# Induced attention and a leaky feed-forward layer on one core: another order of the opening list, the next batch's first loads sent from within it, and longer pauses in two lanes

## The chip, the core and the metric

The kernel runs on one core of a Trainium2 chip. A time is in device microseconds from the start to the end of one execution, and the number to predict is the median of several runs. TensorE multiplies, VectorE and ScalarE work on what it leaves in PSUM, GpSimd does a few elementwise steps, and the queue of SyncE (SP) issues nearly all DMAs, one after the other in the order of the program.

## What is computed

```python
def _attn_ref(x, inducing):              # x (4, 12480, 128), inducing (32, 128)
    def mab(q, kv):
        s = scale * (q @ kv.transpose(0, 2, 1))
        s = s - s.max(-1, keepdims=True)
        a = np.exp(s)
        a /= a.sum(-1, keepdims=True) + 1e-09
        return a @ kv
    h = mab(I, x)                        # 32 rows for each batch
    return mab(x, h)

def _moe_ref(x, w_in, w_out):            # x: the 49920 rows of the attention; w_in (128, 2048), w_out (2048, 128)
    h = x @ w_in
    g = np.maximum(0.01 * h, h)
    return g @ w_out
```

## The kernel before

**Feed-forward part.** The 49920 rows are cut into tiles of 512 tokens, a few of them put together from remainders. For each tile and each of 16 parts of the hidden width there is one *slot*: TensorE makes `ph` from the tile's attention weights `A` and the batch's expanded weights `hws` (L712), ScalarE writes its upper part `ghi` (L725), VectorE what is left over, `glo` (L733), and TensorE adds three products to `po` (L751). After the last part of a tile comes one closing product (L770), then VectorE turns `po` into `osb` (L780), for the first four tiles GpSimd scales it (L783), and SP stores it with four DMAs (L804). `ph` has three buffers, so the `ph` of slot u+3 cannot start before the `glo` of slot u is read out.

**Attention part of a batch.** Per batch there are seven groups of rows: six of 2048 and a remainder of 192. `first_scores` loads blocks `xc` with 32x32 pieces (L250, eight DMAs for a block of half a group, twelve for the remainder; three buffers), VectorE transposes them into `xT` (L391, L397), TensorE scores them against the inducing rows (L264). `fetch` loads the rows `xr` (L222), which give `h` (L440). From `h` come `hws` (L547 to L562) and the second scores; `second` makes their softmax `y` into `aT`, and `stack` splits `aT` into `ahi` (ScalarE, L641) and `alo` (L646) and spreads them with 16 DMAs over four tiles of `A` (L658). There are six `A` buffers: a stack goes on only when its tiles fit beside those still held.

**What sets the order.** Batch 0 up to slot 50 is written by hand: the table `ORDER` names one step after the other, and `start` runs them in that order. `T`, `C` turn and copy a quarter of a group; `S`, `M`, `X`, `N`, `E`, `Y`, `Z`, `H` are scores, maxima, exponentials and products of the first attention; `a`, `b`, `o`, `t`, `p` with a number convert a piece of the raw weights, and `sh`, `sl`, `wt`, `wc`, `wm`, `wd` derive weights from it; `hw`, `wh`, `wl`, `hd` make `hws`; `F`, `G`, `L`, `A`, `B` with a slot's number are `ph`, `ghi`, `glo`, the first and the other two products; `dA2`, `dA3` spread tiles 2 and 3; `os0` to `os2` store a tile; the names that end in `1` (`ymx1` to `yT1`) are the softmax of the second group, and `ah1`, `alo1v`, `dB` drive its stack; `yg2`, `ygR` turn scores of groups 2 and R; `W` is a warm-up product for TensorE's clock (L1217). Tiles 0 and 1 take turns every four slots, so that tile 0 ends with `B27` and tile 1 with `B31`.

From slot 48 on a loop runs the slots and beside them *lanes*, generators that each do a step when their turn comes: stores, `stacking`, `fetches`, `seconds`, `scores` (`first_scores`) and `values`. A step that yields `HEAVY` (15) makes a debt that each slot lowers by 4 or 5, and most lanes wait while there is one. Steps of `fetches` come every second slot. `first_scores` of batch 1 therefore sends its first loads when the loop has begun. `idle(n)` yields n times and does nothing.

All engines execute in the order in which they were written. SP does too: a DMA whose buffer is not free holds all that are behind it.

Of the kernel before, what the change touches and what calls it, by code (L numbers as in the profile page):

```python
# [9 lines left out]
F32 = mybir.dt.float32  # L10
# [10 lines left out]
def induced_attention_then_leaky_ffn(  # L21
# [21 lines left out]
    B, N, C = x.shape  # L43
# [12 lines left out]
    while N - base >= 4 * TOK:  # L56
# [15 lines left out]
    STEPS = [[0, 1, 2], [3, 4], [5, RG]]  # L72

    ORDER = """
        W W W W W indT W W W W T0.1 C0.1v W T0.0 C0.0v W W W T0.2 C0.2a W T0.3 T1.0 C0.3v C1.0v T1.1
        C1.1v S0 M0 T1.3 C1.3a T2.0 T1.2 C1.2v T2.1 C2.0v T2.2 T2.3 C2.3v C2.1a S1 C2.2a S2 M1 T3.1 T3.0
        C3.1a T3.2 M2 X0 C3.2a N0 E0 E2 C3.0v T3.3 T4.1 C3.3v C4.1a T4.2 T4.0 Y0 C4.0v T4.3 C4.2a TR.0 S3
        C4.3a t0 CR.0v S4 E1 a0 M3 T5.0 b0 T5.1 T5.2 M4 X1 Z0 Y1 N1 C5.0a C5.1a T5.3 SR C5.2a al1 H0 o0
        MR C5.3a b1 Y2 a1 o1 p0 S5 t1 p1 H1 H2 M5 X2 E3 Y3 t2 K0 W E4 N2 E5 ER Y4 b2 H3 Y5 H4 a2 Z1 a3
        al2 H5 o2 p2 Z2 z YR K1 HR rz a4 wt1 t3 K2 sr hT t5 b3 hTc b4 o3 p3 s2 o4 sg2 hw y ymx ysubv t4  # L80
        p4 a5 wt0 wt3 wc1 wh wl s21 yex wc0 wm0 yT ah W b5 alov wc3 rep0 rep1 W sh0 J0 J1 o5 ysm hd0 hd1
        hd2 y1 F0 G0 L0 F1 G1 wd0 F2 L1 G2 L2 p5 wm1 sh1 A0 F3 sl0 B0 G3 F4 A1 B1 F5 G4 G5 sl1 A2 a6 L3
        B2 A3 F6 G6 L4 L5 dA3 B3 F7 A4 B4 wt2 ysr G7 L6 L7 t6 A5 B5 b6 F8 wc2 F9 G8 o6 G9 p6 F10 A6 B6 A7
        A8 G10 b7 a7 L8 L9 L10 B7 F11 B8 A9 G11 F12 B9 G12 sc sq A10 B10 L11 L12 F13 o7 G13 t7 A11 A12
        B11 F14 wm2 L13 F15 F16 ymx1 G14 B12 wd1 A13 L14 G15 L15 G16 F17 G17 L16 p7 L17 B13 A14 B14 wm3
        A15 F18 F19 sh2 A16 yg2 G18 sl2 G19 L18 L19 B15 B16 F20 A17 G20 wd2 F21 G21 ysub1g B17 A18 B18
        A19 A20 sh3 F22 B19 G22 L20 L21 B20 A21 wd3 m2 F23 L22 G23 L23 hd3 F24 G24 F25 B21 A22 G25 B22
        L24 sgR F26 mh G26 ml F27 G27 A23 L25 yex1 B23 A24 F28 G28 L26 sl3 B24 A25 F29 B25 G29 A26 B26
        A27 A28 L27 L28 F30 F31 G30 B27 G31 B28 A29 ysm1 L29 L30 dA2 F32 os0 B29 G32 L31 F33 G33 L32 L33
        ysr1 A30 B30 A31 A32 F34 F35 B31 B32 A33 G34 L34 F36 B33 A34 G35 L35 G36 F37 G37 L36 F38 B34 A35  # L90
        B35 A36 L37 F39 F40 G38 L38 G39 L39 B36 F41 G40 G41 A37 L40 B37 A38 B38 A39 F42 F43 G42 G43 L41
        B39 A40 F44 G44 B40 A41 B41 L42 L43 F45 G45 F46 A42 L44 L45 B42 G46 F47 A43 B43 A44 L46 B44 F48
        A45 B45 G47 L47 G48 A46 L48 F49 F50 G49 L49 G50 ymul1g os1 yT1 ah1 alo1v dB B46 A47 B47 os2 L50
        ygR
    """.split()

    QUICK = 2
# [13 lines left out]
    def aux_ps(name):  # L111
        return ps_a.tile([P, TOK], F32, tag="aux", name=name)
# [13 lines left out]
    indT = const.tile([P, M], F32, tag="indT", name="indT")  # L126
# [5 lines left out]
    scores, early, ready, summed = [], {}, set(), {}  # L132
# [4 lines left out]
    xT, xr, ex, aT, A4, hw, maxima, sums_of = {}, {}, {}, {}, {}, {}, {}, {}  # L137
# [88 lines left out]
    def fetch(b):  # L226

        for p, gs in enumerate(PASSES):
            while p and (b, 1) not in visited:
                yield  # L230
            for g in gs:
                for q in range(max(1, GROUPS[g][2] // 4)):
                    while not room():
                        yield
                    load_rows(b, g, q)
                    yield

    def landed(b, p):

# [388 lines left out]
    def stack(tiles_, engine=None):  # L628

        while len(A4) + len(tiles_) > A4_BUFS or not all(s[:2] in aT for t in tiles_ for s in t[1]):  # L630
            yield
        ahi = sb.tile([P, TOK], F32R, tag="ahi", name="ahi", bufs=1)
        alo = sb.tile([P, TOK], F32R, tag="alo", name="alo", bufs=1)
        at = {}
        for _, parts in tiles_:
            for b, g, *_ in parts:
                if (b, g) not in at:
                    at[b, g] = sum(32 * GROUPS[q][2] for _, q in at)
        for (b, g), o in at.items():
            _, J, K = GROUPS[g]  # L640
            nc.scalar.copy(ahi[: 32 * J, o : o + 32 * K], aT[b, g][: 32 * J, :])  # L641
        yield
        for (b, g), o in at.items():
            _, J, K = GROUPS[g]
            sl = (slice(0, 32 * J), slice(o, o + 32 * K))
            (engine or nc.gpsimd).tensor_tensor(  # L646
                out=alo[sl], in0=aT.pop((b, g))[: 32 * J, :], in1=ahi[sl].bitcast(F32),
                op=ALU.subtract,
            )
        yield  # L650
        for t, parts in tiles_:
# [184 lines left out]
    def start(stacking, seconds, chosen):  # L836
# [377 lines left out]
        def warm():  # L1214
# [137 lines left out]
```

## Time and profile before

| | us |
|---|---|
| median of three runs | 1508.52 |
| the runs | 1505.11 to 1508.65 |
| profiled execution | 1507.05 |
| its span | 1505.1 |
| TensorE busy | 1484.8 |
| VectorE busy | 1265.1 |
| ScalarE busy | 997.6 |
| SP: `xc` loads | 288 of 64 KB and 36 of 8 KB |

The span is from the first to the last instruction. The page gives busy times and shares; the timelines give single instructions with, in brackets, how long the engine had been idle before one and what ended that; the table by windows gives busy time and the clock that TensorE was granted (1.00 is 2.4 GHz, 0.50 is 1.2 GHz; a value between is a mean over the window).

### The profile page before, as it was taken

The numbers are of one execution on the slowest core, as the hardware profiler recorded it, in microseconds if no ns is written. First come the engines' busy times: TensorE is split into PE (matmuls) and PEld (weight loads), VectorE is DVE, ScalarE is ACT, GpSimd is POOL, SyncE is SP. The second block draws the span as 40 slices with busy tenths as digits, with TensorE's granted clock in tenths as the row PEclk, the third lists the DMA queues.
The fourth block names the chain that finished last, engine by engine and source line by source line (L and its number), as shares of the span: only waits on it lengthen the run. The fifth ranks groups of instructions, "written<-read, shape, count | busy, mean of one in ns | idle before, by whom it ended". The sixth has DMA issues, their size and how long they took to land.

```text
span 1505.1 us, 22252 instructions
## 1 busy us (share of the span) xinstructions
PE 1484.8 (99%) x7863; PEld 1264.3 (84%) x7863; DVE 1265.1 (84%) x2128; ACT 997.6 (66%) x1746; POOL 116.9 (8%) x186
## 2 busy tenths in 40 slices
PE   8997999999999999999999999999999999999998
PEld 6786888888888888888888888888888898888887
DVE  7886898879898898788899898788888888888886
ACT  5764676667676676676676676676766766666665
POOL 1310000001000000010000000010100000000000
PEclk9998999999999999999999999999999999999999
DMA  8126536434544452244533531221212212212211
GB/s 283 43 50 122 95 60 144 90 47 96 92 90 81 95 108 50 46 84 69 117 64 64 147 61 25 43 64 29 50 27 43 39 31 45 44 25 46 41 28 21
DMA packets 402079, 105.23 MB, mean 70 GB/s; under 512 B 372624, under 2 KB 375088, under 8 KB 401968
## 3 DMA queue, kind: packets, MB, share of 16 engines
q1 hardware_dynamic: 401920, 103.80, 34.2%
q8 instruction: 62, 1.02, 0.3%
q14 instruction: 49, 0.40, 0.1%
q10 hardware_dynamic: 48, 0.02, 0.0%
HBM read 48.94 MB, written 25.56 MB: 49 GB/s over the span
## 4 chain that ended last, share of the span: by engine, by line
PE 94%; DMA 2%; SPq 1%; DVE 1%; ACT 1%; issue 0%; DVEq 0%; ACTq 0%
PE po L751 66%; PE ph L712 22%; PE s_ps L264 2%; PE po L770 1%; DMA xr<-in_x_dram 1%; PE h_ps L440 1%; SPq L250 1%; DMA xc<-in_x_dram 0%; DVE glo L733 0%; PE hw_ps L547 0%; ACT ghi L725 0%; PE h_ps L985 0%; PE w_ps L1085 0%; SPq L658 0%; DVE osb L780 0%
## 5 line engine op out<-in xcount | busy, mean ns | idle before, releaser
L725 ACT ACTIVATE ghi<-ph 128x512 fp32r<-128x512 f32 (+1 forms) x1568 | 928.9, 595 | 475.4 <-PE ph L712 470.6
L733 DVE SCALAR_TENSOR_TENSOR glo<-ph,ghi 128x512 fp32r<-128x512 f32 (+1 forms) x1568 | 1041.5, 679 | 187.5 <-ACT ghi L725 165.4
L712 PE MATMUL ph<-A,hws 128*128 128x512 f32 (+1 forms) x1600 | 596.9, 378 | 10.0 <-DVE glo L733 8.5
L751 PE MATMUL po<-ghi,w_hi 128*128 128x512 f32 (+1 forms) x1568 | 594.4, 380 | 0.4 <-DVE osb L780 0.4
L751 PE MATMUL po<-glo,w_hi 128*128 128x512 f32 (+1 forms) x1568 | 594.2, 379 | 0.0
L751 PE MATMUL po<-ghi,w_lo 128*128 128x512 f32 (+1 forms) x1568 | 594.1, 379 | 0.0
L712 PEld LDWEIGHTS ph<-A,hws 128*128 128x128 f32 x1600 | 302.4, 189 | 70.0 <-DVE glo L733 14.4
L751 PEld LDWEIGHTS po<-ghi,w_lo 128*128 128x128 f32 x1568 | 297.1, 189 | 41.5
L751 PEld LDWEIGHTS po<-glo,w_hi 128*128 128x128 f32 x1568 | 297.2, 190 | 41.3
L751 PEld LDWEIGHTS po<-ghi,w_hi 128*128 128x128 f32 x1568 | 297.1, 189 | 40.5 <-issue 0.8
L780 DVE STREAM_TRANSPOSE osb<-po 128x512 f32<-128x512 f32 (+1 forms) x98 | 68.9, 703 | 1.5 <-PE po L770 1.5
L646 POOL TENSOR_TENSOR alo<-aT,ahi 128x512 fp32r<-128x512 f32 x22 | 28.5, 1296 | 488.2 <-ACT ahi L641 449.0
L397 DVE STREAM_TRANSPOSE xT<-xc 128x512 f32<-128x512 f32 x72 | 50.5, 701 | 8.0 <-DMA xc<-in_x_dram 8.0
L599 POOL TENSOR_TENSOR y<-y,mx 128x512 f32<-128x512 f32 x23 | 24.2, 1052 | 245.4 <-DVE mx L597 220.3
L614 POOL TENSOR_TENSOR y<-y,sm 128x512 f32<-128x512 f32 x23 | 24.2, 1051 | 183.7 <-DVE sm L612 154.8
L770 PE MATMUL po<-A,m2s 128*128 128x512 f32 (+1 forms) x100 | 37.4, 377 | 0.0
L357 DVE STREAM_TRANSPOSE y<-s_ps 128x512 f32<-128x512 f32 x22 | 15.8, 717 | 10.8 <-PE s_ps L264 9.2
L264 PE MATMUL s_ps<-xT,indT 128*32 128x512 f32 x192 | 24.1, 595 | 0.0
L264 PE MATMUL s_ps<-xT,hT 128*32 128x512 f32 x192 | 23.8, 596 | 0.4 <-ACT hT L1029 0.4
L770 PEld LDWEIGHTS po<-A,m2s 128*128 128x128 f32 x100 | 19.0, 190 | 2.6
L282 DVE TENSOR_SCALAR_CACHE_REDUCE e<-s_ps 128x512 f32<-128x512 f32 x18 | 12.4, 691 | 8.3 <-PE s_ps L264 7.5
L440 PE MATMUL h_ps<-xr,ay 128*32 128x128 f32 x576 | 17.6, 274 | 0.0
(161 smaller groups left out, 378.3 us busy)
## 6 DMA issues: line engine op xcount, KB each, us to landing
xr<-in_x_dram SPq DMA_DIRECT2D x96, 256.0 KB, 4.8
out_dram<-osb SPq DMA_DIRECT2D x384, 64.0 KB, 2.2
xc<-in_x_dram SPq DMA_DIRECT2D x288, 64.0 KB, 2.7
A<-ahi SPq DMA_DIRECT2D x188, 64.0 KB, 2.0
A<-alo SPq DMA_DIRECT2D x188, 64.0 KB, 2.0
hws<-hilo SPq DMA_DIRECT2D x64, 64.0 KB, 2.0
raw<-in_moe_w_in_dram SPq DMA_DIRECT2D x4, 512.0 KB, 7.6
raw<-in_moe_w_out_dram SPq DMA_DIRECT2D x4, 512.0 KB, 9.2
```

The lines of the kernel that those rows point to most:

```text
L264: nc.tensor.matmul(dst, lhsT, rhs, start=True, stop=True)
L397: nc.vector.transpose(t[:, j, :], blk.rearrange("p n c -> p (n c)"))
L440: nc.tensor.matmul(hp[32 * k : 32 * k + 32, :C], ay[:rows, 4 * q + k, :], xb[:rows, k, :], start=(i == 0 and q == 0), stop=(last[k] == i a ...
L599: engines[0].tensor_tensor(out=yv, in0=yv, in1=mx[:rows, :K].unsqueeze(2).broadcast_to([rows, K, M]), op=ALU.subtract,)
L614: engines[1].tensor_tensor(out=yv, in0=yv, in1=smv.unsqueeze(2).broadcast_to([rows, K, M]), op=ALU.mult)
L646: (engine or nc.gpsimd).tensor_tensor(out=alo[sl], in0=aT.pop((b, g))[: 32 * J, :], in1=ahi[sl].bitcast(F32), op=ALU.subtract,)
L712: nc.tensor.matmul(ph[:, o : o + w], hw[b][1][:, f * P : (f + 1) * P], woven(A4[t][:, o : o + w], t), start=True, stop=True,)
L725: nc.scalar.activation(halves(ghi[:, :n], t)[1], live[u][2], AF.Relu)
L733: nc.vector.scalar_tensor_tensor(out=halves(glo[:, :n], t)[1], in0=ph, scalar=0.0, in1=halves(ghi[:, :n], t)[1].bitcast(F32), op0=ALU.max, ...
L751: nc.tensor.matmul(accs[t][:, :n], w[:, f, :], woven(r[:, :n], t), start=(f == 0 and w is w_hi and r is live[u][0]), stop=False,)
L770: nc.tensor.matmul(accs[t][:, o : o + w], hw[b][2], woven(a4[:, o : o + w], t), start=False, stop=(o + w == n),)
L780: nc.vector.transpose(osb[:, :n], po[:, :n])
```

## The change

Four edits. The table `ORDER` is written anew from its first row to its last. A new name in it, `pf`, takes the first step of `first_scores` of batch 1, which sends the loads of its first three blocks; so that it can, the generators are made ahead of `start`. `fetch` yields twice after a load instead of once, and `stack` fourteen times at its end instead of three. The numbers of lines after the table are one lower than before.

```diff
@@ ORDER, its end @@
-        A45 B45 G47 L47 G48 A46 L48 F49 F50 G49 L49 G50 ymul1g os1 yT1 ah1 alo1v dB B46 A47 B47 os2 L50
-        ygR
+        A44 B44 A45 F47 F48 G47 L47 B45 A46 G48 F49 B46 A47 L48 F50 G49 G50 B47 L49 os1 L50 ygR os2
@@ ORDER, its middle @@
+        pf mh ml ah1 B27 G28 L28 G29 G30 L29 L30 F31 F32 A28 B28 G31 sq os0 A29 B29 alo1v A30 F33 L31 G32
+        A35 L36 L37 B35 A36 F39 F40 G39 L38 L39 B36 A37 B37 A38 F41 G40 L40 G41 F42 L41 dB B38 A39 B39
@@ fetch @@
                     load_rows(b, g, q)
-                    yield
+                    yield from idle(2)
@@ stack @@
                     to += w
                 yield
-        yield from idle(3)
+        yield from idle(14)
@@ plain @@
+            "pf": lambda: next(scores[0]),
@@ main @@
         stores, values = [], []
+        scores += [first_scores(b) for b in range(1, B)]
         start(stacking[1], seconds[:2], chosen)
         del stacking[:2], seconds[:2]
-        scores += [first_scores(b) for b in range(1, B)]
```

SP, from the spreads of tile 3 to the loop's first blocks, before. `A_1310` is the first tile of the second stack; its 16 spreads are cut after two.

```order
L1172 DMA A_1115<-alo 32x512
L804 DMA out_dram<-osb 512x1x32 x8
L658 DMA A_1310<-ahi 32x512
L658 DMA A_1310<-alo 32x512
...
L804 DMA out_dram<-osb 512x1x32 x4
L250 DMA xc<-in_x_dram 32x2x32 x12
L250 DMA xc<-in_x_dram 32x16x32 x16
L222 DMA xr<-in_x_dram 96x256
L222 DMA xr<-in_x_dram 128x512 x6
L804 DMA out_dram<-osb 512x1x32 x4
L222 DMA xr<-in_x_dram 128x512 x2
L250 DMA xc<-in_x_dram 32x16x32 x16
```

The same stretch of SP in the changed kernel.

```order
L1171 DMA A_907<-alo 32x512
L249 DMA xc<-in_x_dram 32x2x32 x12
L249 DMA xc<-in_x_dram 32x16x32 x16
L803 DMA out_dram<-osb 512x1x32 x4
L657 DMA A_1258<-ahi 32x512
L657 DMA A_1258<-alo 32x512
...
L803 DMA out_dram<-osb 512x1x32 x8
L221 DMA xr<-in_x_dram 96x256
L221 DMA xr<-in_x_dram 128x512 x3
L803 DMA out_dram<-osb 512x1x32 x4
L221 DMA xr<-in_x_dram 128x512
L249 DMA xc<-in_x_dram 32x16x32 x8
```

The 28 loads of the first three blocks have moved ahead of three tiles' stores and of the second stack, and the stores of tiles 1 and 2 behind the stack.

VectorE, from the first tile's store to the end of the list, before (`osb` of tiles 0, 1 and 2; `yr` is the remainder's second score).

```order
L780 STREAM_TRANSPOSE osb<-po 128x512
L733 SCALAR_TENSOR_TENSOR glo<-ph,ghi 128x512 x3
L611 TENSOR_SCALAR sm<-sm 128x16
L612 RECIPROCAL sm<-sm 128x16
L733 SCALAR_TENSOR_TENSOR glo<-ph,ghi 128x512 x16
L780 STREAM_TRANSPOSE osb<-po 128x512
L623 STREAM_TRANSPOSE aT<-y 128x512
L646 TENSOR_TENSOR alo<-aT,ahi 128x512
L780 STREAM_TRANSPOSE osb<-po 128x512
L733 SCALAR_TENSOR_TENSOR glo<-ph,ghi 128x512
L357 STREAM_TRANSPOSE yr<-m_ps 96x64
L733 SCALAR_TENSOR_TENSOR glo<-ph,ghi 128x512
```

The same stretch in the changed kernel, from the second group's `aT` on.

```order
L622 STREAM_TRANSPOSE aT<-y 128x512
L732 SCALAR_TENSOR_TENSOR glo<-ph,ghi 128x512 x4
L527 SCALAR_TENSOR_TENSOR m2s<-m_ps,m2s 64x128
L732 SCALAR_TENSOR_TENSOR glo<-ph,ghi 128x512 x3
L779 STREAM_TRANSPOSE osb<-po 128x512
L732 SCALAR_TENSOR_TENSOR glo<-ph,ghi 128x512 x11
L645 TENSOR_TENSOR alo<-aT,ahi 128x512
L732 SCALAR_TENSOR_TENSOR glo<-ph,ghi 128x512 x2
L356 STREAM_TRANSPOSE y<-s_ps 128x512
L732 SCALAR_TENSOR_TENSOR glo<-ph,ghi 128x512 x6
L779 STREAM_TRANSPOSE osb<-po 128x512
L732 SCALAR_TENSOR_TENSOR glo<-ph,ghi 128x512
```

`aT` has moved ahead of the first tile's store and `alo` to eleven `glo` behind it, and one `glo` stands between the second tile's `osb` and what follows (`yr`, then the third tile's `osb`).

VectorE in the loop, the first blocks of batch 1 and the first transpose that needs the fourth (the fifth `xT`), in the changed kernel; before, the kinds and counts are the same but for the place of one `osb` and one reduction.

```order
L390 STREAM_TRANSPOSE xTr<-xc 128x192
L732 SCALAR_TENSOR_TENSOR glo<-ph,ghi 128x512 x3
L779 STREAM_TRANSPOSE osb<-po 128x512
L732 SCALAR_TENSOR_TENSOR glo<-ph,ghi 128x512 x3
L596 TENSOR_REDUCE mx<-yr 96x2
L732 SCALAR_TENSOR_TENSOR glo<-ph,ghi 128x512 x3
L396 STREAM_TRANSPOSE xT<-xc 128x512
L732 SCALAR_TENSOR_TENSOR glo<-ph,ghi 128x512 x3
L396 STREAM_TRANSPOSE xT<-xc 128x512
...
L396 STREAM_TRANSPOSE xT<-xc 128x512
```

Between the first transpose of a block and the fifth `xT` stand 27 `glo`, three for each heavy step.

## Rows read from the trace of the kernel before

**Rows 1.** The page: the span, and the first line of the busy times

```profile
span 1505.1 us, 22252 instructions
...
PE 1484.8 (99%) x7863; PEld 1264.3 (84%) x7863; DVE 1265.1 (84%) x2128; ACT 997.6 (66%) x1746; POOL 116.9 (8%) x186
```

**Rows 2.** Windows: stretch and length, busy us by engine, granted clock, DMA share, GB/s

```profile
10.00:20.00 10.00, 9.90 (x84) 6.69 (x83) 7.25 (x17) 3.74 (x8) 0.00 (x0) 1.00 1.02 351
20.00:30.00 10.00, 9.39 (x154) 6.05 (x152) 8.40 (x24) 9.24 (x21) 1.91 (x2) 1.00 1.04 375
...
90.00:100.00 10.00, 8.18 (x37) 6.40 (x36) 8.15 (x15) 5.33 (x10) 3.15 (x3) 1.00 0.27 48
...
120.00:130.00 10.00, 7.84 (x23) 5.94 (x24) 5.84 (x11) 3.23 (x7) 0.00 (x0) 0.66 0.59 92
...
140.00:150.00 10.00, 6.31 (x25) 4.97 (x24) 5.01 (x9) 3.71 (x7) 0.78 (x1) 0.88 0.77 132
```

**Rows 3.** Waits of TensorE, whole span: us in total, times, longest

```profile
PE ph L712 <- DVE glo L733: 8.5, 4, 3.7
PE ph L712 <- DVE yr L357: 1.4, 1, 1.4
```

**Rows 4.** Waits of TensorE from 1000 to 1300 us

```profile
PE ph L712 <- DVE glo L733: 0.5, 1, 0.5
```

**Rows 5.** Timeline of VectorE: start, us, instruction, count, idle before it

```profile
120.42 0.38 DVE L391 STREAM_TRANSPOSE xTr<-xc 128x192 f32<-128x192 f32 x1 [4.46 <-DMA xc<-in_x_dram]
...
126.31 0.71 DVE L397 STREAM_TRANSPOSE xT<-xc 128x512 f32<-128x512 f32 x1 [3.73 <-DMA xc<-in_x_dram]
...
146.02 0.71 DVE L397 STREAM_TRANSPOSE xT<-xc 128x512 f32<-128x512 f32 x1 [4.23 <-DMA xc<-in_x_dram]
```

**Rows 6.** Timeline of SP's queue (merged issues)

```profile
56.20 0.59 SPq L1172 DMA_DIRECT2D A<-alo  x1
77.82 17.80 SPq L804 DMA_DIRECT2D out_dram<-osb  x6
...
111.38 18.31 SPq L250 DMA_DIRECT2D xc<-in_x_dram  x28
...
139.10 10.66 SPq L250 DMA_DIRECT2D xc<-in_x_dram  x16
```

**Rows 7.** Timeline of TensorE, `ph` around the two stalls

```profile
116.81 0.38 PE L712 MATMUL ph<-A,hws 128*128 128x512 f32 x1
...
128.62 0.38 PE L712 MATMUL ph<-A,hws 128*128 128x512 f32 x1
...
141.78 0.38 PE L712 MATMUL ph<-A,hws 128*128 128x512 f32 x1
...
142.65 0.38 PE L712 MATMUL ph<-A,hws 128*128 128x512 f32 x1
...
151.10 0.38 PE L712 MATMUL ph<-A,hws 128*128 128x512 f32 x1
```

**Rows 8.** The page, section 6: KB each, median us from issue to landing

```profile
xc<-in_x_dram SPq DMA_DIRECT2D x288, 64.0 KB, 2.7
```

**Rows 9.** Timeline of VectorE at the end of the list

```profile
92.52 0.70 DVE L780 STREAM_TRANSPOSE osb<-po 128x512 f32<-128x512 f32 x1
93.15 0.67 DVE L623 STREAM_TRANSPOSE aT<-y 128x512 f32<-128x512 f32 x1
...
96.32 0.23 DVE L357 STREAM_TRANSPOSE yr<-m_ps 96x64 f32<-96x64 f32 x1
96.47 0.65 DVE L733 SCALAR_TENSOR_TENSOR glo<-ph,ghi 128x512 fp32r<-128x512 f32 x1
```

**Rows 10.** Timeline of ScalarE at the small stack of the last remainders

```profile
1137.48 0.39 ACT L641 CAST ahi<-aTr 96x64 fp32r<-96x64 f32 x2 [1.65 <-DMA A<-ahi]
```

**Rows 11.** Timeline of TensorE in the start: warm-ups and the last quarter-groups' turns

```profile
8.80 0.38 PE L1217 MATMUL warm_ps<-ident 128*128 128x256 bf16 x2
...
23.46 1.92 PE L874 MATMUL xT_ps<-ident,xr 128*128 128x128 f32 x12 [0.39 <-DMA xr<-in_x_dram]
...
31.04 0.38 PE L1217 MATMUL warm_ps<-ident 128*128 128x256 bf16 x2
```

More of the change, by code (lines that the diff above doesn't have):

```diff
@@ L74, in induced_attention_then_leaky_ffn @@
     ORDER = """
[L75 to L89, printed above, removed]
@@ L90, in induced_attention_then_leaky_ffn @@
-        ysr1 A30 B30 A31 A32 F34 F35 B31 B32 A33 G34 L34 F36 B33 A34 G35 L35 G36 F37 G37 L36 F38 B34 A35
-        B35 A36 L37 F39 F40 G38 L38 G39 L39 B36 F41 G40 G41 A37 L40 B37 A38 B38 A39 F42 F43 G42 G43 L41
-        B39 A40 F44 G44 B40 A41 B41 L42 L43 F45 G45 F46 A42 L44 L45 B42 G46 F47 A43 B43 A44 L46 B44 F48
-        A45 B45 G47 L47 G48 A46 L48 F49 F50 G49 L49 G50 ymul1g os1 yT1 ah1 alo1v dB B46 A47 B47 os2 L50
-        ygR
+        W W W W W W W W W W W W W W T0.1 C0.1a W T0.2 C0.2a T0.0 C0.0v W T0.3 indT C0.3a T1.0 C1.0a T1.1
@@ new lines, in induced_attention_then_leaky_ffn @@
+        S0 T1.2 C1.2a C1.1v T1.3 C1.3a T2.0 T2.1 C2.1a T2.2 T2.3 S1 C2.2a C2.0v C2.3a M0 S2 M1 T3.1 C3.1a
+        T3.0 C3.0a M2 T3.3 C3.3a X0 T4.0 N0 E1 E0 C4.0v T3.2 C3.2v T4.1 T4.2 C4.2a T4.3 C4.3a C4.1v Y0 S3
+        S4 Y1 E2 T5.0 t0 M3 M4 C5.0a T5.1 TR.0 a0 C5.1a T5.2 C5.2a X1 b0 T5.3 C5.3a Z0 CR.0v o0 SR MR N1
+        a1 E4 E3 H0 b1 S5 Y2 o1 p0 H1 H2 t1 p1 M5 X2 a2 Y3 K0 t2 N2 E5 al1 ER H3 al2 Y4 H4 a4 a3 b2 Y5 H5
+        o2 p2 Z1 Z2 z YR HR wt0 K1 rz K2 b3 sr b4 o3 t3 p3 hT hTc o4 t4 s2 y wt1 ymx t5 hw ysubv a5 wc0
@@ new lines, in induced_attention_then_leaky_ffn @@
+        wt3 wh wl hd0 yex yT wc1 hd1 hd2 ysm s21 ah p4 sh0 sg2 sl0 wm0 alov wc3 rep0 rep1 ysr wd0 J0 F0
+        y1 F1 J1 W sc G0 b5 o5 F2 L0 hd3 G1 G2 A0 F3 p5 L1 B0 A1 t6 G3 F4 G4 B1 L2 L3 F5 G5 L4 sh1 A2 L5
+        B2 F6 G6 ymx1 ysub1g A3 A4 b6 a7 L6 a6 o6 wm1 p6 F7 G7 B3 wt2 wc2 wd1 F8 G8 L7 L8 B4 A5 sl1 B5 A6
+        F9 G9 L9 sh2 F10 B6 A7 A8 G10 B7 L10 F11 F12 wm2 G11 L11 dA2 F13 G12 dA3 B8 A9 B9 G13 A10 F14 G14
+        L12 L13 L14 B10 F15 G15 L15 F16 A11 A12 b7 B11 G16 B12 A13 F17 F18 G17 L16 L17 B13 A14 B14 F19
@@ new lines, in induced_attention_then_leaky_ffn @@
+        A15 B15 sl2 o7 A16 t7 p7 F20 B16 A17 G18 G19 L18 L19 F21 G20 G21 yex1 wd2 L20 F22 L21 B17 A18 sh3
+        sl3 ysm1 ysr1 F23 ymul1g G22 L22 B18 A19 wm3 B19 A20 G23 F24 G24 B20 A21 B21 F25 wd3 m2 L23 F26
+        yT1 A22 B22 A23 G25 G26 A24 L24 L25 L26 F27 F28 G27 sgR L27 B23 B24 A25 F29 F30 B25 A26 B26 A27
+        pf mh ml ah1 B27 G28 L28 G29 G30 L29 L30 F31 F32 A28 B28 G31 sq os0 A29 B29 alo1v A30 F33 L31 G32
+        L32 G33 L33 B30 A31 F34 F35 B31 F36 G34 A32 B32 L34 G35 G36 L35 A33 B33 F37 F38 G37 A34 G38 B34
@@ L95, in induced_attention_then_leaky_ffn @@
+        A35 L36 L37 B35 A36 F39 F40 G39 L38 L39 B36 A37 B37 A38 F41 G40 L40 G41 F42 L41 dB B38 A39 B39
+        G42 F43 G43 L42 L43 A40 F44 B40 yg2 A41 B41 F45 A42 B42 A43 F46 G44 L44 G45 L45 G46 B43 L46 A44
+        B44 A45 F47 F48 G47 L47 B45 A46 G48 F49 B46 A47 L48 F50 G49 G50 B47 L49 os1 L50 ygR os2
     """.split()
```

## The prediction

> **What bounds the kernel now.** I read the page first: TensorE is busy for 1484.8 of 1505.1 us [rows 1], so time can only come from where it stands still or runs at its lower clock. The busy time by windows says where: 1.8 us idle in 90 to 100, 2.2 us idle and a mean granted clock of 0.66 in 120 to 130, 3.7 us idle and a clock of 0.88 in 140 to 150 [rows 2]. The waits of TensorE name the releaser: VectorE's `glo` four times, 8.5 us in all, and one transpose `yr`, 1.4 us [rows 3]; one of the four, 0.5 us, lies beyond 1000 us [rows 4].
>
> `glo` is not late by its own work. VectorE executes in order, and in front of three of these `glo` stood transposes of the next batch's blocks, which waited 4.46, 3.73 and 4.23 us for their loads `xc` [rows 5]. The loads were late because SP was: only at 111.38 does it come to the 28 `xc` loads of the first three blocks, 18.31 us of issuing, and the next 16 are issued from 139.10. The same SP does nothing between 56.8 and 77.8 [rows 6]. So what ends last from 111 to 146 is SP's queue, through VectorE, on TensorE.
>
> **The two stalls, priced by progress.** One slot of the feed-forward part takes 0.87 us (`ph` at 141.78 and 142.65). From the `ph` at 116.81 to that at 128.62 are five slots: 11.81 us instead of 4.33, a loss of 7.5. From 142.65 to 151.10 are three slots and one closing product, an estimate of 0.22 as a quarter of a slot: 8.45 instead of 2.82, a loss of 5.6 [rows 7]. Together 13.1 us. It contains the half-speed products behind each stall, which the clocks in rows 2 show.
>
> **What the change does to them.** `pf` sends the 28 loads from within the list. On SP they now stand right behind the DMAs of tiles 2 and 3 and ahead of the first tile's stores, as the order of SP shows. They need buffers that last held raw weights. Those of the first two blocks are free early; the third's is read last by `t7`, now behind `A16`, a third of the way through the list: some 65 us. So SP can issue 28 x 0.65 us between 57 and 76, where it does nothing now [rows 6], and with 2.7 us to landing [rows 8] all is there by 79. The first transpose of a block comes at about 118. So the waits at 120.42 and 126.31 go, with nearly 40 us to spare.
>
> The wait at 146.02 is on the next block, whose eight loads can only be sent once a buffer has been transposed out (about 118). On SP they stand behind one tile's stores, which wait for GpSimd until about 120; then four stores, one `xr` and eight loads, 13 x 0.65, and 2.7 to landing give 131. By the order of VectorE 27 `glo` stand between the first transpose and the one that needs them, 27 x 0.87 = 23 us, so about 141. It goes too, with 10 us of cover.
>
> What is late next: I looked at the second stack's tiles. Their first product (slot 64) is ten slots ahead of the `ph` at 116.81 (slot 74), at 108. Their 16 spreads stand behind `pf` and one tile's stores and wait for `dB` at about slot 40, 34 slots ahead of 116.81: 87. They are issued by 98 and have 8 us to spare. Gain 13.1; bounds 7.5 (only the first stall goes) and 13.1.
>
> **The second stack.** `ah1` and `alo1v` stand early in the new list, but the generator finds four tiles held and four wanted against six buffers, and goes on only when tiles 0 and 1 have ended (`B27`, `B31`). So both pass empty and the whole stack is recorded at `dB`. The order agrees: `alo` stands eleven `glo` behind the first store's transpose. What this takes from the list's end is VectorE's heap there: from 92.52 on `osb`, `aT`, `alo`, `osb`, one `glo`, `yr` [rows 9], which costs TensorE 1.4 us of wait [rows 3] in a window with 1.8 idle [rows 2]. There now stand `osb`, `glo`, `yr`, `osb`. That is 1.4 us beside the `glo` (0.63 us from start to start in rows 9 for a transpose, 0.15 for `yr`), where a slot leaves VectorE 0.87 - 0.62 and a `glo` may be about 1 us late before its PSUM buffer is missed (an estimate: three slots of 0.87, less 0.6 for `ghi`, 0.7 for `glo` and 0.3 for the product). `aT`, `alo` and `y` now stand apart, with two or more `glo` between. Gain 1.2, bounds 0 and 1.8.
>
> **More pauses.** `idle(14)` ends every stack. The stacks of four tiles stand in the order at the same slot as before, since they wait for A buffers anyway. Only the small stack of the remainders moves, five slots later: its `ahi` copy at 1137.48 waited 1.65 us for DMAs that still read the buffer, with `ghi` queued behind it on ScalarE [rows 10], and TensorE lost 0.5 [rows 4]. Gain 0.5, bounds 0 and 0.5. `fetch` loads one `xr` every four slots instead of two. The products that need them stand 2 to 5 slots earlier than before on TensorE, and the last batch's weights are ready over 150 slots before its tiles, so a late `xr` delays no product of these; on SP the `xr` now stand between the `xc` loads, which is counted above. 0, bounds 0 and +1.
>
> **The start.** It is rewritten, with the same 17 warm-ups, 14 of them now first, so the first transpose starts near 7.5 instead of 5.5. The later ones wait for the last loads anyway (0.39 us at 23.46) [rows 11], and the order of the DMAs is the same up to there, so that edge stays. From there to the first `ph` near 45 I followed the chain (copies, scores, maximum, exponentials, `h`, scores, softmax, split, spread) through both orders: the same steps, one copy on ScalarE about 0.3 us later, one small product `sc` ahead of slot 2. 0, bounds -1 and +1.5.
>
> **Sum.** The profiled execution took 1507.05 us, 1.95 of it outside the span of 1505.1. Less 13.1, 1.2 and 0.5: 1492.25. It lies 1.5 under the median of the three runs, 1508.52; I add half of that and round: **1493**.
>
> **Rivals.** *One stall stays, or a new one of its size comes*: an `xc` load still late at the fourth block, or a list in which VectorE is late once more. For it: the list's order is new throughout, and TensorE's full busy time today does not show how near to late each `glo` is. Against: the 10 us of cover. It gives back 3 to 6 us: 1496 to 1499.
>
> *The change doesn't do what it says*: SP is held at the third block, since its buffer frees late, and the stores and spreads behind wait too. Had `t7` come 30 us later than I place it, the first transposes would find their loads as late as now: 1503 to 1508. Against: `t7` stands ahead of the product of slot 20.
>
> *Slower than before: the clock of the start.* Fewer warm-ups stand between the first transposes. If TensorE fell to 1.2 GHz there, its work from 10 to 30 us, busy for 9.9 and 9.4 of 10 [rows 2], would take some 20 us more: 1493 + 20 = 1513. It makes the kernel slower than before once it holds for over 15 us. Against: between the warm-ups at 8.80 and 31.04 there are none today [rows 11], only transposes, scores and small products, and the granted clock there is 1.00 [rows 2]. The Trainium skill ("TensorE: Matmul & The Clock Gate", Part 4: PE-mode transpose) says that transposes do not count as busy time for the clock in the same way, which speaks against taking warm-ups from between them; by that rule it would be this rival's 1513. The 1.00 of rows 2 does not bear it out here.
>
> **How the numbers follow.** As forecast (1490 to 1496): 0.72. One stall left or new: 0.17. No effect: 0.05. Slow start: 0.04, three quarters of it at or over 1513. Better than 1490: 0.02. A measurement here tells 0.3%, 4.5 us, from no change, so 1504 to 1513 is "same". Faster 0.91, same 0.06, slower 0.03. The range reaches over the forecast and the second case: 1490 to 1499.
>
> **What will show it.** Right: no transpose of an `xc` block waits for a DMA between 110 and 160, SP issues 28 `xc` loads between 57 and 78, the clock is 1.00 in every window from 50 to 160, and TensorE's waits there are under 2 us. The `ahi` copy of the remainders has no DMA wait. The first `ph` starts between 44 and 46.5. Wrong: a `ph` that waits for `glo` behind a transpose or an `alo`, a first `ph` after 47, or spreads of the second stack that land after 108.

## The result and the profile after

The changed kernel takes 1491.94 us (median of four runs, 1491.70 to 1493.08) beside 1508.58 of the kernel before: a ratio of 0.9897, 95% interval 0.9880 to 0.9914. Forecast were 1493, between 1490 and 1499. The profiled execution took 1492.06 with a span of 1490.0, 15.1 us under that of before [rows 1].

The page, its span and first busy line:

```profile
span 1490.0 us, 22232 instructions
...
PE 1478.1 (99%) x7863; PEld 1261.6 (85%) x7863; DVE 1264.6 (85%) x2123; ACT 1000.8 (67%) x1751; POOL 116.5 (8%) x186
```

Windows of 10 us, columns as in [rows 2]:

```profile
10.00:20.00 10.00, 9.93 (x84) 6.84 (x83) 4.61 (x12) 5.69 (x12) 0.00 (x0) 1.00 1.03 367
20.00:30.00 10.00, 9.09 (x154) 6.13 (x152) 8.87 (x24) 9.33 (x20) 2.11 (x2) 1.00 1.04 368
...
90.00:100.00 10.00, 9.48 (x44) 7.98 (x43) 8.80 (x16) 6.47 (x13) 3.15 (x3) 1.00 0.46 101
...
120.00:130.00 10.00, 10.00 (x48) 8.77 (x47) 9.56 (x18) 7.00 (x13) 0.00 (x0) 1.00 0.73 139
...
140.00:150.00 10.00, 10.00 (x66) 7.34 (x68) 9.19 (x15) 5.37 (x9) 0.00 (x0) 1.00 0.42 104
```

Where TensorE stood 2.2 and 3.7 us at a mean clock of 0.66 and 0.88 [rows 2], it is now busy all the time at 1.00. In 90 to 100 it is idle for 0.5 us instead of 1.8. TensorE's waits over the whole span, of which four are shown, name no `yr` any more, and of the four for `glo` one is left, in the start at 47.45 (against [rows 3]):

```profile
...
PE mx_ps L922 <- DVE onerd L915: 1.0, 1, 1.0
PE xT_ps L873 <- DMA xr<-in_x_dram: 0.8, 2, 0.4
PE ph L711 <- DVE glo L732: 0.7, 1, 0.7
PE po L750 <- DVE osb L779: 0.5, 1, 0.5
...
```

The same `ph` as in [rows 7] (the 76th and 81st, the 97th and 100th, counted from 0) now stand 4.31 and 2.81 us apart, where it was 11.81 and 8.45:

```profile
116.03 0.38 PE L711 MATMUL ph<-A,hws 128*128 128x512 f32 x1
...
120.34 0.38 PE L711 MATMUL ph<-A,hws 128*128 128x512 f32 x1
...
134.37 0.38 PE L711 MATMUL ph<-A,hws 128*128 128x512 f32 x1
...
137.18 0.38 PE L711 MATMUL ph<-A,hws 128*128 128x512 f32 x1
```

SP's timeline (against [rows 6]): the 28 loads now leave right behind the spreads of tiles 2 and 3, and the next groups of eight from 116.85.

```profile
56.53 0.59 SPq L1171 DMA_DIRECT2D A<-alo  x1
57.22 19.46 SPq L249 DMA_DIRECT2D xc<-in_x_dram  x28
78.05 2.67 SPq L803 DMA_DIRECT2D out_dram<-osb  x4
...
96.71 6.12 SPq L803 DMA_DIRECT2D out_dram<-osb  x8
102.88 2.04 SPq L221 DMA_DIRECT2D xr<-in_x_dram  x4
113.55 2.59 SPq L803 DMA_DIRECT2D out_dram<-osb  x4
...
116.85 5.29 SPq L249 DMA_DIRECT2D xc<-in_x_dram  x8
```

VectorE's transposes of the next batch's blocks (against [rows 5]) have no wait; the last row here is the first of the fourth block, whose eight loads had to wait for a free buffer (some texts below call these loads the ninth group). They are issued by 122.1 and, with 2.7 us to landing [rows 8], there at about 125 (an estimate from the two), nearly 8 us ahead of it:

```profile
108.83 0.37 DVE L390 STREAM_TRANSPOSE xTr<-xc 128x192 f32<-128x192 f32 x1
...
116.82 0.70 DVE L396 STREAM_TRANSPOSE xT<-xc 128x512 f32<-128x512 f32 x1
...
132.58 0.70 DVE L396 STREAM_TRANSPOSE xT<-xc 128x512 f32<-128x512 f32 x1
```

At the list's end (against [rows 9]) `aT` and `alo` are gone from between the two `osb`:

```profile
93.52 0.70 DVE L779 STREAM_TRANSPOSE osb<-po 128x512 f32<-128x512 f32 x1
94.15 0.65 DVE L732 SCALAR_TENSOR_TENSOR glo<-ph,ghi 128x512 fp32r<-128x512 f32 x1
94.72 0.23 DVE L356 STREAM_TRANSPOSE yr<-m_ps 96x64 f32<-96x64 f32 x1
94.88 0.67 DVE L779 STREAM_TRANSPOSE osb<-po 128x512 f32<-128x512 f32 x1
```

The small stack of the last remainders comes at 1126.00 and its copy no longer waits for DMAs (1.65 us in [rows 10]):

```profile
1126.00 0.38 ACT L640 CAST ahi<-aTr 96x64 fp32r<-96x64 f32 x2
```

**A yardstick without the start.** Each of the 98 tiles ends with one transpose `osb` on VectorE, and the trace has all 98. The distance from the first to the last leaves out the start, which differs from execution to execution. Before (first fence) and after (second), timeline of VectorE:

```profile
75.96 0.71 DVE L780 STREAM_TRANSPOSE osb<-po 128x512 f32<-128x512 f32 x1
...
1499.20 0.72 DVE L780 STREAM_TRANSPOSE osb<-po 128x512 f32<-128x512 f32 x1 [1.49 <-PE po L770]
```

```profile
75.98 0.72 DVE L779 STREAM_TRANSPOSE osb<-po 128x512 f32<-128x512 f32 x1 [0.19 <-PE po L769]
...
1484.11 0.72 DVE L779 STREAM_TRANSPOSE osb<-po 128x512 f32<-128x512 f32 x1 [1.49 <-PE po L769]
```

1423.24 us before, 1408.13 after: 15.11 less, all of the 15.1 us. All kernels of this study by it (times in us; the last three columns from each kernel's profiled execution):

| kernel | median | first `osb` | first to last `osb` | against before |
|---|---|---|---|---|
| before | 1508.58 | 75.96 | 1423.24 | |
| changed | 1491.94 | 75.98 | 1408.13 | -15.11 |
| changed, once more | 1492.22 | 77.21 | 1408.14 | -15.10 |
| changed, no `pf` | 1495.11 | 75.79 | 1410.65 | -12.59 |
| changed, neither edit | 1504.71 | 75.14 | 1419.60 | -3.64 |
| before + `pf` | 1496.73 | 76.77 | 1412.19 | -11.05 |
| before + early stack | 1501.42 | 75.53 | 1418.09 | -5.15 |
| before + early stack + `fetch` pause | 1498.11 | 76.38 | 1415.06 | -8.18 |
| before + early stack + `pf` behind the spreads | 1494.98 | 76.73 | 1410.44 | -12.80 |
| before, `xc` loads by GpSimd | 1505.44 | 75.24 | 1421.31 | -1.93 |
| changed, short pauses | 1493.49 | 78.36 | 1410.20 | -13.04 |
| changed, no warm-ups | 1492.83 | 76.78 | 1408.15 | -15.09 |
| changed, VectorE steps moved (1) | 1494.50 | 78.74 | 1408.14 | -15.10 |
| changed, VectorE steps moved (2) | 1494.11 | 77.34 | 1408.14 | -15.10 |

Five executions that share everything behind the first tile agree to 0.02 us in the fifth column. The runs of before that stood beside the experiments had medians of 1507.46 to 1507.68. Kernels with stalls vary more from run to run (before 1504.31 to 1509.67, "changed, neither edit" 1502.27 to 1507.46), so their fifth column holds for one execution.

### The profile page after: what moved, and what is told of

The parts are those of the page before. It is cut to its first block, busy times and chain, and to the rows that moved or that the text cites. A ratio compares the mean times of both kernels' runs of the same rounds, so it can differ in the third digit from the quotient of the medians.

```text
span 1490.0 us, 22232 instructions
## 1 busy us (share of the span) xinstructions
PE 1478.1 (99%) x7863; PEld 1261.6 (85%) x7863; DVE 1264.6 (85%) x2123; ACT 1000.8 (67%) x1751; POOL 116.5 (8%) x186
## 3 DMA queue, kind: packets, MB, share of 16 engines
q8 instruction: 62, 1.02, 0.3%
## 4 chain that ended last, share of the span: by engine, by line
PE 96%; DMA 2%; DVE 1%; ACT 0%; issue 0%; DVEq 0%; ACTq 0%
PE po L750 68%; PE ph L711 23%; PE s_ps L263 2%; PE po L769 1%; DMA xr<-in_x_dram 1%; PE h_ps L439 1%; PE hw_ps L546 0%; DMA ind<-in_inducing_dram 0%; DVE glo L732 0%; ACT ghi L724 0%; PE w_ps L1084 0%; PE xT_ps L873 0%; DVE cv_a L1043 0%; DVE ay L957 0%; DVE osb L779 0%
## 5 line engine op out<-in xcount | busy, mean ns | idle before, releaser
L439 PEld LDWEIGHTS h_ps<-xr,ay 128*32 128x32 f32 x576 | 15.2, 110 | 2.9 <-issue 2.6
```

The costliest lines, as they stand in the source:

```text
L439: nc.tensor.matmul(hp[32 * k : 32 * k + 32, :C], ay[:rows, 4 * q + k, :], xb[:rows, k, :], start=(i == 0 and q == 0), stop=(last[k] == i a ...
```

## The experiments

**Which edit carries the gain: four kernels between the two.** My theory was SP's queue from 94 to 140 us: too much to issue in order, so that either edit alone makes room. The rivals: only loads inside the list help; or the rest of the rewriting carries it.

The changed kernel without `pf`:

```diff
-        pf mh ml ah1 B27 G28 L28
+        mh ml ah1 B27 G28 L28
```

> The changed kernel without `pf`: the 28 first `xc` loads are again issued only behind the list; the second stack stays early, so its spreads are out of the way by 97. Theory (SP's queue between 94 and 140 was too full, and either edit alone frees enough of it): the loads go out from about 103 instead of 111 and the second eight-load group from about 125 instead of 139, the first stall shrinks from 7.5 us to at most 2 and the second is gone: 1492 to 1495. Rival (only loads issued within the list help): the transposes of `xc` blocks wait 3 us or more as in the kernel before, and both stalls of 13.1 us stay: 1502 to 1506.

It gave 1495.11 (ratio 0.9918, 0.9903 to 0.9933). That is 0.1 over the range of my theory. SP issues the 28 loads from 103.16; the first transpose waits for nothing and the second for 0.44 us, and TensorE loses nothing there. The ninth group of loads leaves only at 127.99, and a later transpose waits longer:

```profile
135.73 0.71 DVE L396 STREAM_TRANSPOSE xT<-xc 128x512 f32<-128x512 f32 x1 [2.23 <-DMA xc<-in_x_dram]
```

So without `pf` the first stall is gone, and of the second a wait of 1.7 us is left, 2.0 us by the starts of `ph`.

The kernel before with `pf` alone:

```diff
-        A27 A28 L27 L28 F30
+        A27 pf A28 L27 L28 F30
```

> The kernel before with `pf` alone, in its own list behind A27. Theory: the 28 `xc` loads go out by about 80, both stalls (7.5 and 5.6 us) go, and the wait on `yr` at the list's end (1.4 us) and the old remainder stack stay: 1507 - 13.1 = 1494, 1493 to 1496. Rival (the second stack's place or the new order of the list carries the gain): 1500 to 1508.

It gave 1496.73 (0.9927, 0.9910 to 0.9943), 0.7 over my range. All of 110 to 150 is busy at 1.00, so both stalls are gone. But in the old list `A27` stands ahead of tile 2's spreads, and these waited behind 28 loads on SP; TensorE's timeline:

```profile
78.85 0.45 PE L711 MATMUL ph<-A,hws 128*128 128x512 f32 x1 [1.90 <-DMA A<-alo]
```

11.05 us of gain and this new wait of 1.90 make 12.95, close to the 13.1 of the two stalls.

The kernel before with the second stack alone moved:

```diff
+ "ymul1g" behind "ysr1", "yT1" behind "A35", "ah1 alo1v dB" behind "L41"
- "ymul1g", "yT1", "ah1 alo1v dB" behind "G50" at the list's end
```

> The kernel before with its second stack alone moved ahead of the second tile's stores (and the transposes it needs), no `pf`, old pauses. Theory (SP's queue): its 16 spreads are issued from about 87 to 98 instead of behind 94, the 28 `xc` loads from about 99 to 118 instead of 111 to 130, the first stall falls from 7.5 to 0 to 3 us, the second from 5.6 to 0 to 2, and the wait on `yr` is gone: 1492 to 1498. Rival (the loads must leave within the list): both stalls stay, only the list's end gains: 1505 to 1507.

It gave 1501.42 (0.9958, 0.9941 to 0.9974), between the ranges of both theories. SP comes to the 28 loads at 103.58 and the first stall is gone. The second is there in full (7.3 us by the starts of `ph`), and SP issues nine `xr` ahead of the ninth group, which leaves at 132.59:

```profile
139.81 0.71 DVE L396 STREAM_TRANSPOSE xT<-xc 128x512 f32<-128x512 f32 x1 [5.93 <-DMA xc<-in_x_dram]
```

```profile
130.00:140.00 10.00, 5.76 (x27) 4.71 (x25) 3.79 (x7) 4.15 (x7) 0.00 (x0) 1.00 0.72 124
140.00:150.00 10.00, 8.85 (x33) 7.50 (x34) 7.84 (x14) 5.13 (x9) 1.29 (x1) 0.83 0.63 97
```

The changed kernel with both taken back:

```diff
-        pf mh ml ah1 B27 G28 ... os0 A29 B29 alo1v ... F42 L41 dB ... B47 L49 os1 L50 ygR os2
+        mh ml B27 G28 ... os0 A29 B29 ... F42 L41 ... L49 ymul1g os1 yT1 ah1 alo1v dB B47 os2 L50 ygR
```

> The changed kernel with both taken back: no `pf`, and the second stack at the end of the list as in the kernel before; the new order of the rest of the list and the new pauses stay. Theory: both stalls are back, 13 us, with the wait at the list's end: 1503 to 1508. Rival (the other rewriting of the list or the pauses carry the gain): 1491 to 1496.

It gave 1504.71 (0.9980, 0.9971 to 0.9989). The first transposes wait for `xc` for 4.22 and 3.29 us again, and a later one for 2.62. The 28 loads leave at 111.29, as in the kernel before (111.38). The rest of the rewriting with the pauses carries 3.6 us between the profiled executions and 2.9 between the medians (1507.59 for before beside it): 0.8 at the small stack of the remainders, and the rest fits the 2.85 us by which the ninth group leaves earlier (136.25 instead of 139.10), with six `xr` in front of it instead of nine.

**The pause behind the `xr`.** To settle that last point, the early stack in the old list was run with the longer pause in `fetch`:

```diff
                     load_rows(b, g, q)
-                    yield
+                    yield from idle(2)
```

> The kernel before with the second stack early, as in the earlier run of that edit (1501.4), and the longer pause behind each load of `xr` besides. Theory (what is left of the second stall there is SP issuing nine `xr` ahead of the second eight-load group, at 132.6): with fewer `xr` in front that group leaves at 128 to 129, the second stall falls from 5.4 us to about 2, the clock stays at 1.00, and the time is 1496 to 1498. Rival (the rest of the new list is what matters): 1500 to 1502, the stall unchanged.

1498.11 (0.9930, 0.9915 to 0.9944). The ninth group leaves at 129.21 instead of 132.59, the wait for it falls from 5.93 to 3.05 us, and 3.03 us are gained between first and last tile. So here, where loads are late, the pause between unhurried `xr` is worth about the 3.4 us of room that it makes on SP.

**Queue or transfer?** The kernel before, its `xc` loads issued by GpSimd:

```diff
-                nc.sync.dma_start(
+                nc.gpsimd.dma_start(
                     t[32 * cb : 32 * cb + 32, j * K : (j + 1) * K, :],
```

> The kernel before with one edit: the `xc` loads are issued by GpSimd instead of SP, in the same places of the program. Theory (the stalls come from SP's queue, in order, not from the transfers): the first 28 leave before 105, since GpSimd stands free, the transposes no longer wait, the stalls of 13.1 us shrink to 3 at most: 1493 to 1498. Rival (the loads' small pieces or the DMA engines are the limit): they land as late as before, 118 and later, and the time is 1503 to 1510. A third outcome, GpSimd's own work delayed behind its issuing, would show as a wait for `osb` or `scr` on TensorE.

1505.44 (0.9985, 0.9975 to 0.9994). Timelines of GpSimd and VectorE:

```profile
98.12 16.79 POOL L250 DMA_DIRECT2D xc<-in_x_dram  x28
114.92 1.06 POOL L614 TENSOR_TENSOR y<-y,sm 128x512 f32<-128x512 f32 x1
```

```profile
116.02 0.71 DVE L623 STREAM_TRANSPOSE aT<-y 128x512 f32<-128x512 f32 x1 [9.62 <-POOL y L614]
...
126.28 0.37 DVE L391 STREAM_TRANSPOSE xTr<-xc 128x192 f32<-128x192 f32 x1
```

It was the third outcome, though not at the tiles that I had named. No transpose waits for `xc` any more, so the waits came from when the loads were issued. But GpSimd works in order here too: a product of its own (L614) stands behind the 16.8 us of loads, VectorE waited 9.62 us for it, and TensorE stood for 8.9 in one wait. The stall had moved from one queue to another. The transfers are not free either: beside SP's stores and `xr` loads the DMA engines are full (share 1.02 from 110 to 120), and the last of the 28 take up to 8.3 us from issue to landing, against 1.9 to 3.2 in the kernel before.

**Both edits in the old list**, `pf` behind the spreads:

```diff
+ "pf" behind "dA2"; the second stack as in the run with that edit alone
```

> The kernel before, old list and old pauses, with two moves: the second stack early, and `pf` behind the spreads of tile 2 (`dA2`) instead of ahead of them. Theory (these two are the whole of the change, the rest of the rewriting is worth nothing once the loads are early): both stalls and the wait at the list's end go, 1507 - 13.1 - 1.5 = 1492.5, 1491 to 1494.5. Rival (the new order of the list is worth the 4.5 us that stood between the kernel before and the changed one without both edits): 1495 to 1498.

1494.98 (0.9919, 0.9904 to 0.9934), between both ranges: 12.80 of the 15.11 us. No `xc` is waited for. What is missing are 0.8 us near 89, where this list puts `alo` ahead of a `glo` that TensorE needs (a wait of 0.85), and 1.2 and 0.3 us at two small stacks of remainders (near 1128 and 402), whose `ahi` copies wait for DMAs. So the two moves are 85 hundredths of the change; the pauses and the rest of the list are the remainder.

**The pauses in the changed kernel:**

```diff
-        yield from idle(14)
+        yield from idle(3)
...
-                    yield from idle(2)
+                    yield
```

> The changed kernel with the old pauses (3 behind a stack, 1 behind a load of `xr`). Theory of the prediction (the pauses move only the remainder stack): its `ahi` copy near 1125 waits 1.6 us for DMAs again and TensorE loses 0.4 to 0.5 us there; more `xr` stand ahead of the ninth group of `xc` loads on SP, which come 2 to 4 us later, but the transposes had 8 us to spare: 0.3 to 0.6 us over the changed kernel's 1491.9. Rival (the pauses carry part of the gain themselves, as the 4.5 us between the kernel before and the changed one without both edits suggest): a transpose waits for its `xc` near 132 again and the time is 1494 to 1497.

1493.49 (0.9898, 0.9881 to 0.9914). Between first and last tile it loses 2.07 us, more than the 0.3 to 0.6 expected: 1.46 between tiles 71 and 80, where the `ahi` copy waits 2.28 us and TensorE 1.1, and 0.6 between tiles 17 and 26, where the copy of an earlier stack of remainders waits 1.49 us and TensorE 0.33. No transpose waits for `xc`, as the theory said; the time lies between both ranges. ScalarE's timeline:

```profile
401.16 0.39 ACT L640 CAST ahi<-aTr 96x64 fp32r<-96x64 f32 x2 [1.49 <-DMA A<-ahi]
...
1126.84 0.39 ACT L640 CAST ahi<-aTr 96x64 fp32r<-96x64 f32 x2 [2.28 <-DMA A<-ahi]
```

**The start: clock and warm-ups.** The changed kernel without its 17 warm-ups:

```diff
-        W W W W W W W W W W W W W W T0.1 C0.1a W T0.2 ... W T0.3 ... J1 W sc
+        T0.1 C0.1a T0.2 ... T0.3 ... J1 sc
```

> The changed kernel without any of its 17 warm-ups. Theory (the start waits for the loads, and transposes and scores keep the clock up as the products do): the granted clock reaches 1.00 by 10 to 15 us, cost 0 to 3 us: 1492 to 1495. Rival (the Trainium skill, TensorE: Matmul & The Clock Gate, Part 4: PE-mode transposes do not count as busy time for the clock in the same way): the clock stays at 0.50 until the scores or later, 30 us, and the time is 1500 to 1513.

1492.83 (0.9906, 0.9890 to 0.9923), 0.6 over the changed kernel beside it (1492.22), and the runs of the two overlap (1492.61 to 1493.93, 1491.06 to 1493.30). TensorE's timeline:

```profile
5.17 3.99 PE L873 MATMUL xT_ps<-ident,xr 128*128 128x128 f32 x16 [5.17 <-DMA xr<-in_x_dram]
...
9.59 1.97 PE L873 MATMUL xT_ps<-ident,xr 128*128 128x128 f32 x8 [0.19 <-DMA xr<-in_x_dram]
11.49 1.94 PE L263 MATMUL s_ps<-xT,indT 128*32 128x512 f32 x8
13.35 3.19 PE L873 MATMUL xT_ps<-ident,xr 128*128 128x128 f32 x24
```

A transpose takes 0.25 us up to 11.5 and eight scores 1.94 (1.06 at 11.04 in the changed kernel); from 13.35 a transpose takes 0.13, the full rate (2.4 GHz). The column of the granted clock reads 1.00 all through this stretch, so it doesn't show a half rate that was never raised; the durations do. 24 transposes alone did not bring the full rate, and it stood right after the first eight scores. That agrees with the Trainium skill ("TensorE: Matmul & The Clock Gate", Part 4: PE-mode transpose), by which transposes do not count as busy time for the clock in the same way. It is one execution, and whether the scores or only the time raised the rate is not shown. The price here is some 0.6 us, not clear of the noise, and not the 20 of my rival. The start waits for its loads: at 23.93 ten transposes of the changed kernel stand behind a wait of 0.44 us for an `xr`, and without warm-ups the same ten and the four ahead of them run from 24.01 without one. The first tile ends at 76.78, between the 75.98 and 77.21 of two executions with warm-ups.

**Once more, and two tries for a better start.** In the changed kernel small VectorE steps of the start take some 1.2 us beside an operation of GpSimd (last section). The first try moved them behind others:

```diff
-  o1 p0 H1 H2 t1 p1 M5 X2 a2 Y3 ... rep1 ysr wd0 J0 F0 y1 F1 J1 W sc G0 b5 o5 F2 L0 hd3 G1 G2 A0 F3
+  p0 H1 H2 t1 M5 X2 a2 Y3 o1 p1 ... rep1 wd0 J0 F0 F1 J1 W G0 F2 L0 ysr y1 hd3 G1 b5 o5 G2 A0 F3 sc
```

> The changed kernel with small VectorE steps moved out of the way of GpSimd in the start: `ysr`, `y1` behind the first slot's `glo`, the split `b5`, `o5` behind the second slot's product, `sc` later, and `o1`, `p1` behind the third maximum step. Theory (a VectorE instruction on a shared path waits until GpSimd's running two-input operation has ended, so that an operation of 0.16 us took 1.27): the 0.74 us wait for `glo` at 47.45 goes, the sum's small step behind `L0` takes under 0.3 us, the maximum's step at 29.2 takes 0.2 instead of 1.26, and the time is 0.5 to 1.5 us under the changed kernel: 1490.4 to 1491.4. Rival (these operations are slow by themselves there): they take 1.2 us at their new place too and the time is that of the changed kernel or longer.

The steps became as short as the theory said (0.16 and 0.17 us), and the kernel slower: 1494.50 (0.9907, 0.9892 to 0.9921). `apart`, which spreads the sum's inverse, now stands behind the splits on VectorE, and `sc` on TensorE waits for it. That wait, and windows of TensorE around it and behind it (busy us, granted clock, DMA share, GB/s):

```profile
PE sc_ps L1132 <- DVE apart L1125: 1.6, 1, 1.6
```

```profile
45.00:50.00 5.00, 3.11 (x11) 0.88 0.42 102
50.00:55.00 5.00, 5.00 (x24) 0.78 0.40 100
```

The second try kept the move of `o1`, `p1` and gave the others more distance, with the changed kernel beside it:

```diff
-  rep1 ysr wd0 J0 F0 y1 F1 J1 W sc G0 b5 o5 F2 ... F3 p5 L1 B0 A1 t6 ... L3 F5 ... F6 G6
+  rep1 wd0 J0 F0 F1 J1 ysr y1 W G0 F2 ... F3 L1 B0 A1 b5 t6 ... L3 o5 F5 p5 ... F6 G6 sc
```

> The changed kernel with the sum's small step `ysr`, `y1` behind the next scores' transpose, the splits `b5` and `o5` behind the third and fourth slot's `glo`, `sc` behind slot 6, and `o1`, `p1` behind the third maximum step. Theory (GpSimd's operation holds VectorE up, and nothing else of the start hangs on these steps): the sum's step takes under 0.3 us, the first `glo` stands 0.5 to 0.8 us sooner, no wait on `sc` as in the run with `sc` early, clock 1.00: 0.5 to 1.0 us under the changed kernel. Rival (VectorE's whole work before slot 6 sets the pace): the wait for `glo` comes a few slots later, and the time is the changed kernel's, within 0.3.

> The changed kernel once more, beside the three others of this call. Theory: the list's part ends as in the first profile, 1491.5 to 1493.5; what varies between executions is the start, where a late `xr` near 24 can let TensorE's clock fall. Rival (the first result was a lucky one): 1494 or more.

1494.11 (0.9913, 0.9898 to 0.9927) against 1492.22 (0.9900, 0.9886 to 0.9915) of the changed kernel once more, whose theory held. The wait for the first `glo` fell from 0.7 to 0.2 us, but the sum's step fell beside GpSimd again (43.57, 1.27 us), and `sc` waits 1.43 at 51.19. So the second try's theory failed, and its rival (the changed kernel's time within 0.3) too: it is 1.9 over. The order that spares one wait makes another; that VectorE's whole work sets the pace there is likely, but not shown. Neither try beats the changed kernel.

## Why the prediction was right, step by step

- **The two stalls, 13.1 us.** Right in mechanism and size: 7.50 and 5.64, together 13.14. That SP's queue was the cause is shown three ways: early loads take the waits for `xc` away, another queue does too, and of the third wait that an early stack leaves (5.93 us) a pause that frees SP by 3.4 us takes away half.
- **`pf` on SP, 57 to 76.** It issues from 57.22 to 76.68, behind the spreads of tiles 2 and 3, as the order said. That this place mattered the prediction didn't price: the same `pf` ahead of the spreads cost 1.90 us in the old list.
- **The next block, 131 against 141.** It was there at about 125 and needed at 132.58: 8 us of cover instead of 10. I had both ends 6 to 8 us too late: the first block's transpose, which frees the buffer, came at 108.83 and not at 118, and the tile's stores ahead of the loads at 113.55 and not at 120.
- **The second stack's spreads, 87 to 98.** Issued from 86.39 to 96.6. Their first product starts at 105.45 and not at 108, since the `ph` at 116.81 in [rows 7] is that of slot 76, not 74; the cover of some 7 us was enough.
- **The list's end, 1.2, and the start, 0.** The wait for `yr` is gone, but the list's end is worth 0.8 and not 1.2: from the first tile's end to the `ph` of slots 56 to 76 the changed kernel gains 0.8. The first tile ends at 75.98 (75.96 before), as forecast; that is partly luck, since other executions of the same start end it 1.2 and 2.4 us later. Of the 15.11 us behind the first tile, 0.8 are the list's end, 13.14 the stalls, 0.84 the remainder stack (125.26 us from the 71st to the 80th `osb` before, 124.42 after), and 0.3 come in steps of about 0.1 between the slots 100 and 1071, with no wait beside them.
- **The pauses, 0.5 with bounds 0 and 0.5.** The one term that was too small: 0.84 against the kernel before, and 2.07 in the changed kernel when the pauses alone are taken back. I priced the wait that I saw (0.5) and took it for the bound, but a wait costs more than the idle time shown:

```profile
1139.15 0.48 PE L712 MATMUL ph<-A,hws 128*128 128x512 f32 x1 [0.49 <-DVE glo L733]
```

  The `ph` ahead of it starts at 1137.62, so 1.53 us lie between the two instead of a slot's 0.87: 0.66 lost. A product is shown with 0.38 us while the next starts 0.22 behind it, and idle time counts from the product's end. Two starts behind it come 0.10 and 0.07 late, which makes the 0.83. With short pauses in the changed kernel a wait of 1.12 costs 1.46 in the same way. There the copy waits longer than before (2.28 us instead of 1.65), and the earlier stack of remainders, which I took for unmoved, loses 0.6. I also gave `fetch` nothing; beside `pf` no transpose waits for `xc` with either pause; without `pf` the longer one is worth 3 us.
- **One stall stays or a new one comes.** It did not: the ninth group had nearly 8 us of cover. That cover is `pf`'s: without it the group is 2.23 us late.
- **The slow start.** Not with 20 us. A small form of it is real: in two executions of the same start (the changed kernel once more, and short pauses) TensorE waited 1.67 us until 9.37 and 1.42 us until 26.07 for an `xr`, and its granted clock then fell to 0.50 for some 3 us (0.50 from 11 to 14 and from 27 to 29). Between its last warm-up or score and the fall it had done transposes alone, with that wait among them. The first tile then ended at 77.21 and 78.36 instead of 75.98. My reading of the granted clock in [rows 2] as evidence against the rule of the Trainium skill was too short: it shows that the clock was kept between scores, not that transposes keep it.

1493 against 1491.94: the sum of 1492.25 stood 0.2 above the profiled 1492.06, and half of the distance to the median, which I added, was not needed. That the sum is so close is partly luck: the list's end was 0.4 too large, the pauses 0.3 too small, and for the 0.3 of small steps the sum had no term.

What stays open: the steps of about 0.1 us without a wait, 0.3 us here and 0.5 of the 2.5 that the kernel without `pf` loses.

## What to carry to other kernels

When loads come late, look first at what the issuing queue does ahead of them, and for an idle stretch of that queue before the rush; moving the issue there was worth the whole 13.1 us here, and moving it to another in-order engine moved the stall to that engine's own work. Price a move by every queue that it passes, and where it stands against what is already urgent there: 28 loads one place too early cost 1.9 us. Price a wait by the starts of the products around it and not by the idle time shown: here 0.49 us of idle time cost 0.83. To compare executions whose start differs, measure between two landmarks of which the trace has every record.

## What the runs showed of the hardware

**GpSimd holds some instructions of VectorE up, whatever their size.** Timelines of VectorE and GpSimd in the changed kernel, and of VectorE in the first try, where GpSimd's operation no longer stands beside:

```profile
29.21 1.26 DVE L915 TENSOR_TENSOR onerd<-onerm,own 128x8 f32<-128x8 f32 x1
...
43.50 1.27 DVE L1120 TENSOR_SCALAR sm<-sm 128x16 f32<-128x16 f32 x1
```

```profile
29.18 1.27 POOL L1059 TENSOR_TENSOR w_in_sb<-cv_a,cv_t 128x512 int32<-128x512 int32 x1 [2.09 <-DVE e L906]
...
43.45 1.29 POOL L1066 TENSOR_TENSOR w_lo<-wraw,w_hi 128x512 fp32r<-128x512 f32 x1 [3.32 <-ACT w_hi L1062]
```

```profile
28.93 0.17 DVE L915 TENSOR_TENSOR onerd<-onerm,own 128x8 f32<-128x8 f32 x1
...
46.27 0.16 DVE L1120 TENSOR_SCALAR sm<-sm 128x16 f32<-128x16 f32 x1
```

Eight or sixteen columns took 1.26 and 1.27 us, as long as GpSimd's operation that had begun 0.03 and 0.05 us earlier; at another time they take 0.17 and 0.16. Other executions show that what they wait for is its end: `onerd` took 0.80 us in the kernel before (from 29.88, beside GpSimd's 1.27 from 29.39) and 1.16 without warm-ups (from 30.10, beside 1.27 from 29.97), and each time it ended 0.02 us behind GpSimd's operation. The Trainium skill ("GPSIMD Engine Reference", 1. Specifications) states that GpSimd shares its SBUF interfaces with VectorE, with contention for VectorE instructions in a 2-port mode or with two SBUF inputs; `onerd` has two inputs and agrees. The sum's step has one, and no run here shows its mode. The hold is up to a whole GpSimd operation here. A transpose of VectorE beside GpSimd (38.02, 0.72 us) was not held up.

**A wait of TensorE in the start can cost twice**, once as the wait and once as products at half rate behind it, as the two executions with a late `xr` and the first try (1.6 us of wait, then a mean clock of 0.88 and 0.78 over 10 us) show. It need not: behind the second try's wait of 1.43 us at 51.19 the granted clock stayed at 1.00.
